# One PSUM tensor per bank in place of one per two banks, in a linear-attention and mixture-of-experts kernel

**Chip, cores, metric.** One core of a Trainium2 chip. The metric is the device time of one execution in microseconds (us). Before the change three runs gave 286.63 to 290.11 us, median 289.97. Every run here carries the profiler's records of span and clock, so nothing in this document tells how the kernel runs without them.

## The reference, cut to what matters

```python
# attention with a decaying state; r, k, v, w of shape (4, 8, 768, 48)
for t in range(S):
    y[:, :, t] = r_t @ (state + (u * k_t) outer v_t)
    state = w_t[..., None] * state + k_t outer v_t
x = y as 3072 tokens of 384
# every token to one of 8 experts, highest logits first, each expert full at 384 tokens
logits = x @ w_gate
...
for e in range(E):
    h = maximum(x[mask] @ w1[e], 0)          # 384 -> 1024
    out[mask] = h @ w2[e]                    # 1024 -> 384
```

## The kernel before

The attention runs in 24 units of 128 tokens (about 20 to 165 us). The experts follow in two passes: 256 tokens each, from a token list made while the last attention units still run, and then 128 tokens each. For every 128 tokens GpSimd issues an indirect DMA that gathers rows (L1076), and later one that scatters results (L1168). It also issues the weight loads (L1024, L1026). TensorE turns the gathered rows (L1087), multiplies by w1 (up, L1117), ScalarE (in the second pass also VectorE) applies the ReLU (L1134, L1132), TensorE multiplies by w2 (down, L1148), and the result is copied out of PSUM (L1161, L1158). Four PSUM banks go round among up and down products. They are the halves of two tensors, which the attention uses first:

```python
    Cps = ps.tile([128, 1024], FP32, name="cps", tag="cps")        # two banks
    Gps = ps.tile([128, 2, 512], FP32, name="gps", tag="gps")      # two banks: the grams
    # ... (cut) the attention: grams by TensorE, then masks by VectorE
                    mm(Gps[cols, cc, j * 64:(j + 1) * 64], lhsT=t[rows, j, 0, cols],
                       rhs=t[rows, j, 1, cols], start=True, stop=True)
                nc.vector.copy_predicated(out=M[slot(("m", u))][:, cc], mask=...,
                    data=Gps[:, cc, :256].rearrange("p (j t) -> p j t", j=NPAIR))
    # ... (cut) the experts
        views = {"T": list(Tps), "D": [Yps[:, 0], Yps[:, 1]],
                 "B": [Cps[:, :512], Cps[:, 512:], Gps[:, 0], Gps[:, 1]]}
    # ... (cut) up, ReLU, down, copy; self.bank("B", key) is one of the four
                            nc.tensor.matmul(
                                self.bank("B", b[1])[:, i * size:(i + 1) * size],
                                lhsT=w1sb[:, k, f8 * 128:(f8 + 1) * 128], rhs=xv()[:, k],
                                start=(k == 0), stop=(k == 2))
                        nc.scalar.activation(out=to, in_=of, func=AF.Relu)
    # ... (cut)
                    got = nc.gpsimd.indirect_dma_start(
                        out=self.xg[slot[xg[1]]], out_offset=None, in_=self.x_dram,
                        in_offset=bass.IndirectOffsetOnAxis(ap=tok[:, j:j + 1], axis=0))
```

Of the kernel before, what the change touches and what calls it, by code (L numbers as in the profile page):

```python
# [8 lines left out]
FP32 = mybir.dt.float32  # L9
# [8 lines left out]
B, H, S, D = 4, 8, 768, 48  # L18
# [4 lines left out]
E = 8  # L23
# [4 lines left out]
NPAIR = 4  # L28


def _bc(ap, n, pos=None):

    pat = [list(x) for x in ap.ap]
    pat.insert(len(pat) if pos is None else pos, [0, n])
    return bass.AP(tensor=ap.tensor, offset=ap.offset, ap=pat)


def _free(ap, *pattern):

    return bass.AP(tensor=ap.tensor, offset=ap.offset,  # L40
                   ap=[list(ap.ap[0])] + [list(x) for x in pattern])
# [38 lines left out]
class Line:  # L80
# [10 lines left out]
    def add(self, name, u, *a, **kw):  # L91
        op = Op(name, u, *a, **kw)
        self.ops.append(op)
        self.op[name, u] = op
        return op
# [176 lines left out]
FREE = {"LG": -2, "LE": -2, "LT": -2, "LF": -2}  # L272


def _attention(tc, inp, sb, ps, r, k, v, w, uu, wg, x_dram, negl, consts, stores):

    nc = tc.nc
    NB = 2
# [27 lines left out]
    Wd = tiles(sb, "wd", 2, [128, NPAIR, B])  # L306
    LS = tiles(sb, "ls", 2, [128, 128])

    Cps = ps.tile([128, 1024], FP32, name="cps", tag="cps")
    Tps = [ps.tile([128, 512], FP32, name=f"tps{i}", tag=f"tps{i}") for i in range(2)]  # L310
    Tb = [t.bitcast(BF16) for t in Tps]
    Gps = ps.tile([128, 2, 512], FP32, name="gps", tag="gps")
    Yps = ps.tile([128, 2, 512], FP32, name="yps", tag="yps")

    Cx = Cps[:, 128:896].rearrange("p (x n) -> p x n", x=2)
# [3 lines left out]
    def mm(*a, **kw):  # L319
        ln.last = nc.tensor.matmul(*a, **kw)  # L320
# [16 lines left out]
    def zero(name, i, engine, ns, ap):  # L337
# [5 lines left out]
    zw = [zero("Zw", i, "POOL", 150, t[:, :, D:]) for i, t in enumerate(Ws)]  # L343
    zs = zero("Zs", 0, "POOL", 500, St[0])
    zg = [add("Zg", i, "DVE", 300,
              lambda i=i: nc.vector.memset(Gps[32:64 if i == 0 else 128, :, 256:448]
                                           if i == 0 else Gps[96:128, :, 256:448], 0.0))
          for i in range(2)]
    zy = [add("Zy", i, "DVE", 400,
              lambda i=i: nc.vector.memset(Yps[32 + 64 * i:64 + 64 * i, :, :256], 0.0))  # L350
# [77 lines left out]
    for u in range(NU):  # L428
# [4 lines left out]
        def cum(ww=ww, b=b):  # L433
# [31 lines left out]
            give=[("dg", u)],  # L465
# [5 lines left out]
        for half in range(2):  # L471
# [11 lines left out]
            def ev(u=u, half=half):  # L483
# [6 lines left out]
                give=[("t", u, half)], **kw)  # L490

        def state(u=u, vv=vv, b=b):
            s = KR[slot(("kr", u))]
            for j in range(NPAIR):
                for half, cc in ((0, 0), (1, 1), (0, 1), (1, 0)):
                    h = 2 * j + cc
                    rows = slice(half * 64, half * 64 + 64)
                    mm(Gps[cc * 64:cc * 64 + D, half, 256 + j * D:256 + (j + 1) * D],
                       lhsT=s[rows, 0, h, :D],
                       rhs=vv[rows, b, h * D:(h + 1) * D], start=True, stop=True)  # L500

# [2 lines left out]
            take=("G", ("gu", u)), give=[("kr", u)])  # L504

        def u_of(half):
            return Gps[:112, half, 256:256 + NPAIR * D].rearrange("p (j d) -> p j d", d=D)

        add("SM", u, "DVE", 357, after=[op["U", u], get("SW", u - B), zs],
            take=("Sm", ("sm", u)), give=[("gu", u)],  # L510
            fn=lambda u=u, c=c, b=b: nc.vector.tensor_tensor(
                out=Sm[slot(("sm", u))][:112], in0=u_of(0), in1=St[c % 2][:112, b],
                op=ALU.add))
        if not last_c:
            add("SP", u, "DVE", 357, after=[op["SM", u]], take=("Sp", ("sp", u)),
                give=[("gu", u)],
                fn=lambda u=u: nc.vector.tensor_tensor(
                    out=Sp[slot(("sp", u))][:112], in0=u_of(1),
                    in1=Sm[slot(("sm", u))][:112], op=ALU.add))
            add("SW", u, "POOL", 600, after=[op["SP", u], op["WE", c * B + B - 1],  # L520
                                            get("Y1", u - B)],
                give=[("sp", u)],
                fn=lambda u=u, c=c, b=b: nc.gpsimd.tensor_tensor(
                    out=St[(c + 1) % 2][:112, b], in0=Sp[slot(("sp", u))][:112],
                    in1=_free(Wd[c % 2][:112, 0, b:b + 1], [B, NPAIR], [0, D]),
                    op=ALU.mult))
# [19 lines left out]
        def gram(u=u):  # L546
            t = KRT[slot(("krt", u))]
            for j in range(NPAIR):
                for cc, half in ((0, 0), (1, 1), (0, 1), (1, 0)):
                    rows, cols = slice(cc * 64, cc * 64 + D), slice(half * 64, half * 64 + 64)  # L550
                    mm(Gps[cols, cc, j * 64:(j + 1) * 64], lhsT=t[rows, j, 0, cols],
                       rhs=t[rows, j, 1, cols], start=True, stop=True)
        add("G", u, "PE", 580, gram, mode="Q", lag=120, take=("G", ("g", u)),
            after=krt_ops + [op["IA", u]])
        for cc in range(2):
            add(f"MS{cc}", u, "DVE", 440, after=[op["G", u], op["DG", u]], give=[("g", u)],
                fn=lambda u=u, cc=cc: nc.vector.copy_predicated(  # L557
                    out=M[slot(("m", u))][:, cc], mask=_free(mask, [0, NPAIR], [1, 64]),
                    data=Gps[:, cc, :256].rearrange("p (j t) -> p j t", j=NPAIR)))

        for cc in range(2):
            def intra(u=u, vv=vv, b=b, inter=inter, cc=cc):
# [13 lines left out]
                give=[("m", u), ("krt", u), ("sm", u)] if cc else ())  # L576
# [39 lines left out]
        if b == B - 1:  # L616
            def logits(c=c):
# [8 lines left out]
                give=[("xf", u - i) for i in range(B)])  # L626
# [43 lines left out]
EARLY = 20  # L670
# [8 lines left out]
class Deal:  # L679
# [98 lines left out]
    def early(self, tok, a1, *after):  # L778


        nc, c = self.nc, self.c
        last = self.own(0, EARLY, *after)
        nm2 = self.t("fm", [128, NTILE, E])
        non = self.t("non", [128, NTILE, E], BF16)
        m8, m8b = self.t("m8", [96, 2, 8]), self.t("m8b", [(EARLY - GI) * E, 8])
        (wa, wb), (num, end) = self.worst([(m8[:, 0], 0, GI), (m8b, GI, EARLY)], "T", last,
                                          sums=EARLY)
        self.early_worst = wa
        ready = self.V(EARLY * E, lambda: nc.vector.scalar_tensor_tensor(
            out=nm2[:, :EARLY], in0=non[:, :EARLY], scalar=BIG, in1=self.nl[:, :EARLY],  # L790
            op0=ALU.mult, op1=ALU.add), last)
        key = self.key()
        mean = lambda: self.bank("T", key)[:E, :8]

        def means():
            for i, (of, rows) in enumerate(((m8[:, 0], GI * E), (m8b, (EARLY - GI) * E))):
                nc.tensor.matmul(mean(), lhsT=c["mean8"][:rows], rhs=of, start=(i == 0),
                                 stop=(i == 1))
        p = self.P(130, means, wa, wb, take=("T", key))
        pen, cut, q1 = self.t("pen8", [E, 8]), self.t("cut", [E, 8]), self.t("q1", [E, 1])  # L800
        v = self.V(8, lambda: nc.vector.tensor_scalar(
            out=pen, in0=c["steps"], scalar1=num, scalar2=float(EARLY * 128 - KEEP + 10),
            op0=ALU.add, op1=ALU.is_gt), end)
        v = self.V(8, lambda: nc.vector.scalar_tensor_tensor(
            out=cut, in0=pen, scalar=BIG / 2, in1=mean(), op0=ALU.mult, op1=ALU.add), v, p,
            give=[key])
        v = self.V(8, lambda: nc.vector.tensor_reduce(out=q1, in_=cut, axis=AX.X,
                                                      op=ALU.min), v)
        qb, key, p = self.bound(q1, "T", v)
        asg = self.t("asg", [128, NTILE, E], BF16)  # L810
        v = self.tt(asg[:, :EARLY], nm2[:, :EARLY], lambda: _bc(qb(), EARLY, 1), ALU.is_le, p,
                    ready, give=[key], n=EARLY * E)
        return self.slots(asg, a1, EARLY, FIRST, tok, "T", v)

    def slots(self, asg, mine, n, size, tok, pool, *after, verify=None):
# [575 lines left out]
def kernel(  # L1391
# [12 lines left out]
    nc = tc.nc  # L1404
    x_dram = nc.dram_tensor("x_scratch", (N, DX), BF16, kind="Internal").ap()
# [3 lines left out]
    inp = ctx.enter_context(tc.tile_pool(name="inputs", bufs=1))  # L1409
# [4 lines left out]
    negl = keep.tile([128, NTILE, E], FP32, name="negl", tag="negl")  # L1414
# [9 lines left out]
    with ExitStack() as work, tc.manual_schedule():  # L1424
        nc.scalar.preload_act_table_set("natural_log_exp_and_others")
        consts, later = _constants(tc, const)
        sb = work.enter_context(tc.tile_pool(name="work", bufs=1))
        ps = work.enter_context(tc.tile_pool(name="psum", bufs=1,
                                             space=bass.MemoryType.PSUM))
        stores = []  # L1430
        line, ins, (Cps, Tps, Gps, Yps) = _attention(
            tc, inp, sb, ps, r, k, v, w, u, moe_w_gate, x_dram, negl, consts, stores)
        op = line.op
        fixed = line.plan(lambda o: o.u * PERIOD + AT[o.name])
        assert fixed, "the keys lead to a deadlock"
# [32 lines left out]
        for i, (engine, ns, fn) in enumerate(later):  # L1468
# [2 lines left out]
        line.pools.update(B=4, D=2, FXG=Experts.XG, FXE=Experts.XE, FHS=Experts.HS,  # L1471
                          FOS=Experts.OS)
        views = {"T": list(Tps), "D": [Yps[:, 0], Yps[:, 1]],
                 "B": [Cps[:, :512], Cps[:, 512:], Gps[:, 0], Gps[:, 1]]}

        def bank(pool, key):
            return views[pool][line.slot[key]]
        deal = Deal(nc, line, bank, sb, consts, negl, "D", 20 * 16)
        deal.flag = flag
        zero = deal.step("POOL", 200, lambda: nc.gpsimd.memset(a1[:, EARLY:], 0.0))  # L1480
# [31 lines left out]
    with tc.If(more > 0):  # L1512
        tok = keep.tile([128, NTILE], I32, name="tok", tag="tok")
        with ExitStack() as a:
            sb = a.enter_context(tc.tile_pool(name="b_sb", bufs=1))
            ps = a.enter_context(tc.tile_pool(name="b_ps", bufs=1,
                                              space=bass.MemoryType.PSUM))
            line = Direct()
# [38 lines left out]
```

## Time and profile before

| | before |
|---|---|
| three timed runs | 289.97, 286.63, 290.11 us |
| profiled run | 272.1 us (span 270.2, mean clock 0.933) |
| TensorE busy | 81% of the span; no other engine over 55% |
| first pass of the experts | 168.1 to 237.4 us |
| second pass | 237.4 to 262.3 us |

The last two rows run, to within 0.4 us, from the first up product to the last down product of a pass. Keep an eye on the first two: the profiled run is 18 us shorter than the timed ones. The prediction shows the lines.

### The profile page before, as it was taken

Reading aid. Unit: us, or ns where it says so; the run is one execution under the profiler, and the core shown is the slowest. Engines: PE = TensorE matmul, PEld = TensorE weight load, DVE = VectorE, ACT = ScalarE, POOL = GpSimd, SP = SyncE. Lnnn points to the kernel's source line nnn. Section 1 sums busy time; section 2 is a strip of 40 time slices with the busy share of each in tenths; the row PEclk is TensorE's granted clock in tenths of the full one; section 3 lists DMA queues with packets and bytes.
Section 4 is the critical chain, followed back from the end, with each engine's and each line's share of the span. In section 5 each row is a group of like instructions: output and inputs, shape, how many; then the busy total and the mean of one; then the engine's idle time right before and its main releaser. Section 6 shows DMA issues by size and latency. Waiting matters only on the chain.

```text
span 270.2 us, 10431 instructions
## 1 busy us (share of the span) xinstructions
PE 219.8 (81%) x4469; PEld 162.0 (60%) x4469; DVE 144.9 (54%) x438; ACT 131.9 (49%) x248; POOL 148.4 (55%) x180
## 2 busy tenths in 40 slices
PE   2089998898999799879679589888887789899980
PEld 0057766676677587657467367465555656577850
DVE  6846675575667566555387861264543383024440
ACT  2137676575677577556445223374444454542300
POOL 7425577455757557845735358164752452776331
PEclk9999999999999999997799755599999999999995
DMA  7957799678869769999997994996999599443111
GB/s 155 192 116 135 144 177 202 120 153 182 177 127 205 155 128 196 197 202 138 168 220 142 182 163 83 207 194 151 184 177 225 112 202 187 120 142 105 58 65 63
DMA packets 118388, 42.24 MB, mean 156 GB/s; under 512 B 101440, under 2 KB 113728, under 8 KB 118336
## 3 DMA queue, kind: packets, MB, share of 16 engines
q1 hardware_dynamic: 104128, 21.84, 40.0%
q0 software_dynamic: 14208, 19.66, 38.3%
q8 instruction: 37, 0.61, 0.9%
q14 instruction: 15, 0.12, 0.1%
HBM read 46.61 MB, written 7.47 MB: 200 GB/s over the span
## 4 chain that ended last, share of the span: by engine, by line
PE 66%; issue 11%; DVE 10%; ACT 6%; POOL 4%; POOLq 0%; DVEq 0%; ACTq 0%
PE yps L320 12%; PE gps L320 8%; PE cps L320 6%; PE tps L320 6%; PE gps L1117 6%; PE cps L1117 6%; PE tps L478 5%; PE cps L1148 5%; PE gps L1148 5%; ACT Fhs L1134 3%; DVE mm L557 3%; PE tps L590 2%; POOL out_dram L1168 2%; DVE Dohl L870 1%; PE tps L1087 1%
## 5 line engine op out<-in xcount | busy, mean ns | idle before, releaser
L466 POOL TENSOR_TENSOR mm<-diag,dd 128x512 f32<-128x512 f32 x24 | 25.1, 1046 | 59.0 <-DVE dd L461 23.0
L484 ACT COPY krT<-tps 112x512 f32<-112x512 f32 x48 | 28.1, 586 | 26.5 <-PE tps L478 23.5
L1168 POOL DMA_INDIRECT out_dram<-Fos,tok x24 | 24.1, 1005 | 24.3 <-ACT Fos L1161 11.5
L1076 POOL DMA_INDIRECT Fxg<-x_scratch,tok x24 | 23.4, 975 | 22.4 <-PE tps L1087 12.0
L320 PE MATMUL cps<-ww,negut 128*128 128x384 f32 x48 | 23.7, 579 | 12.3 <-issue 7.2
L478 PE MATMUL tps<-ident,krs 128*112 128x128 f32 x192 | 32.2, 295 | 0.6 <-DVE Dboth L710 0.6
L557 DVE COPY_PREDICATED mm<-mask,gps 128x256 f32<-128x256 uint8 x48 | 18.7, 442 | 22.1 <-PE gps L320 16.3
L478 PEld LDWEIGHTS tps<-ident,krs 128*112 128x112 f32 x192 | 23.0, 142 | 11.1 <-issue 6.1
L1148 PEld LDWEIGHTS <-Fhs 128*128 128x128 bf16 x192 | 17.8, 97 | 13.0 <-issue 3.5
L453 POOL TENSOR_TENSOR rku<-kr 128x384 f32<-128x384 f32 x24 | 24.0, 1002 | 2.6 <-DMA kr<-in_r_dram 2.6
L457 POOL TENSOR_TENSOR rku<-rku,u_bc 128x384 f32<-128x384 f32 x24 | 24.0, 1002 | 2.4 <-DMA u_bc<-in_u_dram 2.4
L320 PE MATMUL yps<-mm,vv 64*48 64x64 f32 x768 | 20.5, 234 | 4.9 <-issue 3.2
L320 PE MATMUL yps<-krT,sm 48*48 48x64 f32 x384 | 22.2, 233 | 1.9 <-issue 1.8
L447 DVE TENSOR_TENSOR krs<-kr,cps 128x768 f32<-128x768 f32 x24 | 22.7, 945 | 1.6 <-ACT cps L442 1.6
L320 PEld LDWEIGHTS yps<-mm,vv 64*48 64x48 f32 x768 | 15.0, 127 | 13.7 <-DVE mm L557 5.9
L578 ACT COPY xf<-yps 128x512 f32<-128x512 f32 x24 | 14.0, 582 | 16.8 <-PE yps L320 12.6
L320 PE MATMUL yps<-krT,st 48*48 48x64 f32 x384 | 21.9, 233 | 0.0
L442 ACT ACTIVATE cps<-cps 128x768 f32<-128x768 f32 x24 | 19.3, 804 | 5.2 <-DVE cps L438 5.2
L1117 PEld LDWEIGHTS <-w 128*128 128x128 bf16 x192 | 15.7, 103 | 9.2 <-issue 6.3
L1134 ACT ACTIVATE Fhs<-cps 128x512 bf16<-128x512 f32 x20 | 11.9, 597 | 18.1 <-PE cps L1117 17.9
L1134 ACT ACTIVATE Fhs<-gps 128x512 bf16<-128x512 f32 x20 | 11.9, 597 | 14.6 <-PE gps L1117 14.4
L320 PEld LDWEIGHTS yps<-krT,sm 48*48 48x48 f32 x384 | 15.6, 128 | 4.8 <-issue 3.6
(200 smaller groups left out, 473.8 us busy)
## 6 DMA issues: line engine op xcount, KB each, us to landing
w<-in_moe_w_dram POOLq DMA_DIRECT2D x8, 768.0 KB
ww<-in_w_dram SPq DMA_DIRECT2D x24, 192.0 KB, 3.7
kr<-in_k_dram SPq DMA_DIRECT2D x24, 192.0 KB, 3.8
kr<-in_r_dram SPq DMA_DIRECT2D x24, 192.0 KB, 4.1
vv<-in_v_dram SPq DMA_DIRECT2D x24, 192.0 KB, 3.8
kr<-in_moe_w_dram POOLq DMA_DIRECT2D x4, 768.0 KB
x_scratch<-row SPq DMA_DIRECT2D x7, 384.0 KB, 4.8
vv<-in_moe_w_dram POOLq DMA_DIRECT2D x2, 768.0 KB
```

The lines of the kernel that those rows point to most:

```text
L320: ln.last = nc.tensor.matmul(*a, **kw)
L453: fn=lambda u=u, kr=kr, b=b: nc.gpsimd.tensor_tensor(out=P[slot(("p", u))], in0=kr[:, b, 0, :], in1=kr[:, b, 1, :], op=ALU.mult))
L457: fn=lambda u=u: nc.gpsimd.tensor_tensor(out=P[slot(("p", u))], in0=P[slot(("p", u))], in1=u_bc, op=ALU.mult))
L466: fn=lambda u=u: nc.gpsimd.tensor_tensor(out=M[slot(("m", u))], in0=_free(diag, [0, 2], [0, NPAIR], [1, 64]), in1=_free(Dg[slot(("dg", u)) ...
L478: ln.last = nc.tensor.transpose(t[:112, at:at + 128], pair_of(s[:, x], j), ident)
L484: nc.scalar.copy(out=KRT[slot(("krt", u))][:112, 2 * half:2 * half + 2].rearrange("p j x t -> p (j x t)"), in_=Tps[slot(("t", u, half))][: ...
L557: fn=lambda u=u, cc=cc: nc.vector.copy_predicated(out=M[slot(("m", u))][:, cc], mask=_free(mask, [0, NPAIR], [1, 64]), data=Gps[:, cc, :25 ...
L1076: got = nc.gpsimd.indirect_dma_start(out=self.xg[slot[xg[1]]], out_offset=None, in_=self.x_dram, in_offset=bass.IndirectOffsetOnAxis(ap=to ...
L1117: nc.tensor.matmul(self.bank("B", b[1])[:, i * size:(i + 1) * size], lhsT=w1sb[:, k, f8 * 128:(f8 + 1) * 128], rhs=xv()[:, k], start=(k == ...
L1134: nc.scalar.activation(out=to, in_=of, func=AF.Relu)
L1148: nc.tensor.matmul(self.bank("B", b[1])[:, :DX], lhsT=hv()[:, f8, h * 128:(h + 1) * 128], rhs=w2sb[:, f8, :], start=(f8 == 0), stop=(f8 == ...
L1168: put = nc.gpsimd.indirect_dma_start(out=self.out, out_offset=bass.IndirectOffsetOnAxis(ap=tok[:, j:j + 1], axis=0), in_=self.os[slot[o[1] ...
```

## The change

The built program orders every access to a tensor, so a ReLU that reads bank 0 of `Cps` stands between two groups of products into bank 1. The change gives every bank a tensor of its own. The two halves of `Cps` are used as one by the attention, so that tensor lives in a pool that is closed when the experts first ask for a bank, and two one-bank tensors take its place.

```diff
-    Cps = ps.tile([128, 1024], FP32, name="cps", tag="cps")
+    Cps = pc.tile([128, 1024], FP32, name="cps", tag="cps")
-    Gps = ps.tile([128, 2, 512], FP32, name="gps", tag="gps")
+    Gps = [ps.tile([128, 512], FP32, name=f"gps{i}", tag=f"gps{i}") for i in range(2)]
 ... (every Gps[x, cc, y] becomes Gps[cc][x, y]; a key's name and the pools' set-up are cut)
         views = {"T": list(Tps), "D": [Yps[:, 0], Yps[:, 1]],
-                 "B": [Cps[:, :512], Cps[:, 512:], Gps[:, 0], Gps[:, 1]]}
+                 "B": [None, None] + Gps}
         def bank(pool, key):
-            return views[pool][line.slot[key]]
+            i = line.slot[key]
+            if views[pool][i] is None:
+                wide.__exit__(None, None, None)
+                new = work.enter_context(psum("psum_c2"))
+                views[pool][:2] = [new.tile([128, 512], FP32, name=f"cps{x}", tag=f"cps{x}")
+                                   for x in range(2)]
+            return views[pool][i]
```

## The prediction

> **What bounds the kernel now.** I read the table of the page first (TensorE busy 81%, no other engine over 55%), then busy time by stage, then the waits inside the stage that looked loose, then the chain that ended last, in that stage.
>
> ```profile
> core 0: us, PE busy (x) PEld busy (x) DVE busy (x) ACT busy (x) POOL busy (x), PEclk, DMA share, GB/s
> 20.00:135.00 115.00, 103.68 (x3052) 79.50 (x3051) 69.61 (x167) 74.70 (x139) 72.53 (x84) 0.97 0.85 165
> 135.00:167.00 32.00, 25.10 (x646) 19.69 (x644) 21.31 (x72) 11.72 (x24) 16.64 (x19) 0.76 0.88 163
> 167.00:200.00 33.00, 27.65 (x187) 17.95 (x186) 14.85 (x69) 15.62 (x31) 17.38 (x19) 0.87 0.98 180
> 200.00:235.00 35.00, 29.18 (x249) 20.16 (x248) 14.59 (x72) 16.56 (x32) 16.30 (x18) 1.00 0.90 171
> 235.00:252.00 17.00, 16.36 (x188) 12.59 (x187) 6.02 (x11) 5.76 (x11) 11.42 (x12) 1.00 0.36 116
> ```
>
> The attention (20 to 135) keeps TensorE busy 90% of the time. The experts come in two passes: 256 tokens each (about 168 to 237), where TensorE stands still for 11.2 of 68 us, and 128 tokens each (from 238), where it hardly stands still at all (16.36 of 17). So the first pass is where something can be won. Its waits, from 167 to 252:
>
> ```profile
> ACT Fhs L1134 <- PE cps L1117: 13.1, 16, 2.4
> ACT Fhs L1134 <- PE gps L1117: 13.0, 17, 2.3
> ...
> PE cps L1117 <- ACT Fhs L1134: 3.0, 4, 0.7
> PE gps L1117 <- ACT Fhs L1134: 2.9, 4, 0.7
> ...
> PE gps L1117 <- ACT Fos L1161: 1.5, 3, 0.6
> ...
> PE cps L1148 <- ACT Fhs L1134: 1.5, 3, 0.6
> ...
> PE cps L1117 <- ACT Fos L1161: 1.2, 2, 0.6
> ...
> PE gps L1148 <- ACT Fhs L1134: 0.8, 2, 0.6
> ```
>
> TensorE waits for ScalarE 18 times, 10.9 us in all: nearly all of its idle time. ScalarE in turn waits for TensorE, and has only 32.2 us of work in those 68. Neither is short of capacity; they take turns. First two lines of the timeline there (start, length, engine, instructions), then three of the chain (start, length, what), show one such turn:
>
> ```profile
> 203.12 1.15 PE L1117 MATMUL cps<-Fxe,kr 128*128 128x256 bf16 x9
> ...
> 204.37 0.60 ACT L1134 ACTIVATE Fhs<-cps 128x512 bf16<-128x512 f32 x1 [0.39 <-PE cps L1117]
> ```
> ```profile
> 203.29 1.00 PE cps L1117 x9
> ...
> 204.37 0.61 ACT Fhs L1134
> ...
> 205.01 0.49 PE cps L1117 x3
> ```
>
> Nine matmuls are six that fill one bank and three for half of the next bank; then the ReLU of the first bank; then the other three. With four banks there should be no such turn.
>
> **What the Trainium skill says.** "PSUM — Partial Sum Buffer", section "PSUM bank collisions raise a hardware error", says that two engines collide only in the same bank and quadrant, that accesses to different banks run clean, and that a semaphore is to guard a bank. So a wait of TensorE on a read of the neighbouring bank guards nothing; the trace shows such waits, 10.9 us of them. "Perfetto Trace Analysis", section "Matmuls", wants independent groups to rotate through banks so that the evacuation of one lies beside the next group's matmuls; the schedule rotates over four, but the chain shows no overlap. "DMA: Bandwidth & Descriptors", section "Anatomy of one DMA — SWDGE (gpsimd) path", fits 2.0 us plus bytes over 436 GB/s: for one weight load here (384 x 1024 fp32, 1.57 MB read) an estimate of 5.6 us. The trace agrees: the packets of one load span 5.0 to 7.1 us.
>
> **The change part by part.** Built side by side, both programs have the same instructions in the same order on every engine, except that VectorE has four small memsets of the gram banks for two. What differs is who waits for whom.
>
> Start: the two memsets took 378 ns each; four halves cost at most some 0.3 us more, at the beginning of VectorE's queue. Estimate +0.2.
>
> Attention: the grams and state products alternate between the two banks, so the last matmuls into both are neighbours. The masks (MS0) and state sums may now start one matmul earlier, some 30 ns (32 matmuls in 0.85 us), and are followed by the same wait one instruction later. VectorE gets 27 waits more. The one gram wait that moves (on the state sum) moves by one matmul. Estimate 0.
>
> First pass: in the program of before, the second half of a bank's products waits for the ReLU or copy of the other bank of the same tensor, and that ReLU waits for the first half. In the changed one it waits only for its own bank, last used four groups ago. The down products (L1148), which belong to the expert before, waited for the last ReLU of the current one and now wait for a ReLU three ScalarE instructions earlier. All 18 waits are of these two kinds, so 10.9 us go. Each also drains the pipeline: nine matmuls in 1.15 us with 0.27 for one are (1.15 - 0.27) / 8 = 0.11 apart, so the next could have started at 204.11 where it started at 205.01. That is 0.90 lost where 0.74 is shown as idle; 0.16 x 18 = 2.9 more. Sum 13.8 us out of the pass's 69.3.
>
> Check by work: an expert has 24 up products at 0.11 (2.64), 16 down products at (1.46 - 0.326) / 7 = 0.162 (2.59), six transposes at 0.055 (0.33) and a round of the token assignment between them (0.31 + 0.40 + 0.42 = 1.13): 6.7 us. Now an expert takes 9.4 (192.33 to 201.70 to 211.11). ScalarE has 4 x 0.60 + 4 x 0.48 = 4.3 per expert, about 4.7 with gaps, so it keeps up with 6.7.
>
> Second pass: 3.0 us per expert (243.79 to 246.79) with TensorE full. Its cross-bank waits go as well, but they end before TensorE arrives. Estimate 0. The tail after the last matmul (262 to 270) is unchanged.
>
> **The rivals, which eat part of the 13.8.**
>
> Weights. Eight loads for experts 4 to 7 run from 178.7 to 231.6, their packets covering 46.6 us of it, at a DMA share of 0.9 or more. Today they are issued by GpSimd in step with TensorE and start about 2 us after issue; the last lands at 231.6 and is used at 234.81. If TensorE is 13.8 earlier it wants it at 221.0, but starting at about 178 with no gap between them, 178 + 46.6 = 224.6. That is a new wait of 3.6 us, on the DMA. For: shares of 0.98 and 0.90. Against: idle gaps at 185 to 187 and 213 to 215. If the DMA could not be compressed at all, the gain would be only 234.81 - 231.6 = 3.2 us, and the time 287.
>
> Token assignment. Its small matmuls sit in TensorE's order, so TensorE waits if VectorE isn't done. A round needs about 2.55 (L723 to L755), 1.75 (to L966) and 2.6 or 1.9 (back to L723): 6.9 or 6.2 against the 6.7 of work. Today VectorE waits for TensorE in it. I take off 1.0 us in all.
>
> GpSimd. From 228 to 248 it issues gathers and scatters without a pause, 1.28 us each, and begins when the second token list is ready, itself late in the assignment. The transposed rows of the second pass could come up to 1 us late. I take off 0.5. If gathers queue behind weight loads it would be 3 or more.
>
> ScalarE as the new bound is the fourth; 4.7 against 6.7 speaks against it, and it would leave a gain above 10.
>
> **Range and chances.** 13.8 - 3.6 - 1.0 - 0.5 + the start's -0.2 = 8.5, rounded to 9 because the overlapped loads at 215 to 231 took 5.5 each and not 5.8. The timed runs (289.97) are some 18 us longer than the profiled one (272.1); I assume that the gain carries over whole, since the wait is ScalarE's latency and not TensorE's speed: 289.97 - 9 = 281.0. All of the rivals at their worst leave about 3 (287), none of them 14 (276). Range 276.0 to 286.0. Two per cent is 5.8 us, a time under 284.2. Faster 0.75, within 2% 0.23, slower 0.02: no wait is added that takes the place of a shorter one.
>
> **What would show it.** Right: no waits of TensorE for Fhs or Fos in the first pass (under 2 us of 10.9); six, not nine, matmuls before a ReLU; expert period near 6.9; new waits of TensorE on weights, at experts 6 or 7; the pass shorter by 8 to 11; the attention and the second pass within 1 us each. Wrong: the pass still near 69 because the DMA or the assignment fills the holes (then waits on weights or VectorE of over 8 us), or a shorter pass whose gain is lost before the second pass because the second token list or its gathers are late, or a granted clock that falls where TensorE is fuller (1.00 from 176 to 264 now).

## The result, and the profile after

The changed kernel took 266.54, 266.9, 270.41 and 264.71 us, median 266.72; the kernel before, in the same rounds, a median of 288.3. The ratio is 0.9344 [0.9166, 0.9522]. (A run counts as slow when it is over 1.5% above the fastest of its kernel. Here and below a ratio is the mean time of one kernel's fast runs over that of the other's fast runs of the same rounds, so not quite the ratio of the medians quoted.) That is 21.6 us less in the medians and 18.7 less in the means of the fast runs. The prediction had 9 and held 14 for out of reach.

Profile against profile the change looks much smaller: 272.1 us before, 266.54 after. These rows give the two passes: window, length, then busy us and count of TensorE, its weight loads, VectorE, ScalarE and GpSimd, then clock, DMA share, GB/s. Before:

```profile
168.10:237.40 69.30, 58.30 (x443) 38.75 (x441) 29.30 (x139) 32.50 (x63) 34.67 (x37) 0.95 0.92 174
237.40:262.30 24.90, 24.12 (x282) 18.60 (x279) 10.60 (x20) 7.07 (x13) 12.96 (x14) 1.00 0.29 97
```

After:

```profile
171.40:227.30 55.90, 53.11 (x445) 37.39 (x443) 28.93 (x139) 32.00 (x63) 33.34 (x36) 1.00 1.00 197
227.30:256.80 29.50, 25.49 (x281) 19.01 (x279) 10.49 (x19) 7.08 (x13) 13.67 (x15) 0.94 0.23 81
```

The first pass is 13.4 us shorter, close to the 13.8 that the waits promised. (In part that is luck: the first expert of before took 9.2 us in this profile, where the pass had a clock of 0.95, and 6.6 in a later profile of the same kernel at 1.00.) But the pass starts 3.3 us later and the second takes 4.6 us more; TensorE is idle for 4.0 of its 29.5. All 18 waits for ScalarE in the first pass are gone. What TensorE waits for in that pass now (us in total, times, longest):

```profile
PE gps L1117 <- DMA vv<-in_moe_w_dram: 1.6, 1, 1.6
PE yps L966 <- DVE Dmm L710: 1.0, 1, 1.0
```

And the turn of nine, ReLU, three has become six for one bank, with the next twelve under the ReLU (the timeline after: start, length, engine and instructions):

```profile
204.07 0.82 PE L1117 MATMUL cps<-Fxe,vv 128*128 128x256 bf16 x6
...
204.73 1.47 PE L1117 MATMUL gps<-Fxe,vv 128*128 128x256 bf16 x12
204.99 0.60 ACT L1134 ACTIVATE Fhs<-cps 128x512 bf16<-128x512 f32 x1 [0.19 <-PE cps L1117]
```

So the mechanism was the predicted one. Two things were not explained: where the timed runs of before spend the 18 us that its profile does not show, and why the change takes some of them away.

### The profile page after: what moved, and what is told of

It is laid out like the page before. It is cut to its first block, busy times and chain, and to the rows that moved or that the text cites. A ratio compares the mean times of both kernels' runs of the same rounds, so it can differ in the third digit from the quotient of the medians.

```text
span 264.6 us, 10437 instructions
## 1 busy us (share of the span) xinstructions
PE 215.1 (81%) x4469; PEld 160.1 (61%) x4469; DVE 142.9 (54%) x440; ACT 131.3 (50%) x248; POOL 148.6 (56%) x180
## 4 chain that ended last, share of the span: by engine, by line
PE 68%; DVE 8%; DMA 8%; issue 7%; another core or an unknown queue 3%; ACT 3%; POOL 2%; POOLq 0%; DVEq 0%
PE yps L320 11%; PE tps L478 8%; PE gps L320 7%; PE tps L320 7%; PE cps L320 7%; PE gps L1117 6%; PE gps L1148 6%; PE cps L1117 6%; PE cps L1148 5%; DMA vv<-in_moe_w_dram 4%; DMA ww<-in_w_dram 3%; PE tps L590 2%; PE tps L1087 1%; DVE Dohl L870 1%
## 5 line engine op out<-in xcount | busy, mean ns | idle before, releaser
L466 POOL TENSOR_TENSOR mm<-diag,dd 128x512 f32<-128x512 f32 x24 | 25.1, 1048 | 57.5 <-DVE dd L461 31.1
L1168 POOL DMA_INDIRECT out_dram<-Fos,tok x24 | 24.1, 1003 | 24.7 <-DVE Fos L1158 13.7
L1076 POOL DMA_INDIRECT Fxg<-x_scratch,tok x24 | 23.5, 977 | 20.3 <-PE tps L1087 11.1
L557 DVE COPY_PREDICATED mm<-mask,gps 128x256 f32<-128x256 uint8 x48 | 18.7, 442 | 27.9 <-PE gps L320 16.7
L478 PE MATMUL tps<-ident,krs 128*112 128x128 f32 x192 | 31.5, 290 | 0.6 <-DVE Dboth L710 0.6
L478 PEld LDWEIGHTS tps<-ident,krs 128*112 128x112 f32 x192 | 22.7, 140 | 10.9 <-issue 6.2
L320 PE MATMUL yps<-mm,vv 64*48 64x64 f32 x768 | 19.9, 232 | 9.0 <-DVE mm L557 6.0
L1148 PEld LDWEIGHTS <-Fhs 128*128 128x128 bf16 x192 | 17.8, 99 | 11.9 <-issue 2.8
L320 PE MATMUL yps<-krT,sm 48*48 48x64 f32 x384 | 21.6, 229 | 1.1 <-issue 1.1
L320 PE MATMUL yps<-krT,st 48*48 48x64 f32 x384 | 21.3, 228 | 0.3 <-issue 0.3
L320 PE MATMUL gps<-krT 48*64 48x64 f32 x768 | 18.4, 227 | 1.0 <-issue 1.0
L1134 ACT ACTIVATE Fhs<-cps 128x512 bf16<-128x512 f32 x20 | 11.8, 598 | 13.8 <-PE cps L1117 10.3
L1117 PEld LDWEIGHTS <-w 128*128 128x128 bf16 x192 | 15.1, 100 | 5.8 <-issue 4.1
```

Source lines behind the costliest of these rows:

```text
L320: ln.last = nc.tensor.matmul(*a, **kw)
L466: fn=lambda u=u: nc.gpsimd.tensor_tensor(out=M[slot(("m", u))], in0=_free(diag, [0, 2], [0, NPAIR], [1, 64]), in1=_free(Dg[slot(("dg", u)) ...
L478: ln.last = nc.tensor.transpose(t[:112, at:at + 128], pair_of(s[:, x], j), ident)
L1076: got = nc.gpsimd.indirect_dma_start(out=self.xg[slot[xg[1]]], out_offset=None, in_=self.x_dram, in_offset=bass.IndirectOffsetOnAxis(ap=to ...
L1117: nc.tensor.matmul(self.bank("B", b[1])[:, i * size:(i + 1) * size], lhsT=w1sb[:, k, f8 * 128:(f8 + 1) * 128], rhs=xv()[:, k], start=(k == ...
L1148: nc.tensor.matmul(self.bank("B", b[1])[:, :DX], lhsT=hv()[:, f8, h * 128:(h + 1) * 128], rhs=w2sb[:, f8, :], start=(f8 == 0), stop=(f8 == ...
```

## The experiments

Fifteen runs were made, in four sets, each on one chip with runs of the kernel before in the same rounds.

| set | chip | kernel before, median (runs) |
|---|---|---|
| 1 | 15 | 286.07 us (11) |
| 2 | 11 | 269.0 us (11) |
| 3 | 2 | 289.51 us (7) |
| 4 | 10 | 288.02 us (7) |

The chips differ as much as the kernels do; that became the key to the case. Medians here and below include slow runs; where times are subtracted, the means of fast runs are used. The kernel before has 283.6, 265.8, 286.4 and 286.6 us in the four sets by that measure. The profiles of before_sp, b_burst, after_third, b_burst_again and pause_all are of slow runs.

### Set 1: where the 18 us are, and which half of the change counts

Theory A: the extra time of the timed runs lies outside the first pass. Rival B: it lies in the first pass, whose waits are longer than in the one profile.

**b_again**, the kernel before, unchanged, profiled once more.

> The kernel before, unchanged, once more. Its three early runs took 287 to 290 us but its profiled run only 272, while the changed kernel's runs and its profile agree (265 to 270). Theory A (the gain is the cross-bank waits of the first expert pass, about 13.5 us in the traces, and the rest of the 21.6 us is a slower condition of the kernel before that its one profile missed): the runs spread over 270 to 290 and a profile near 285 shows extra time outside the first pass, or a lower granted clock. Rival B (the waits cost more in the timed runs than in the profile): a profile near 285 shows the same stages, with the first pass near 78 us and not 69.

284.13 us, 0.9924 [0.9816, 1.0033] of itself in other runs, so a difference of 1% means nothing here. Its two passes:

```profile
172.50:240.30 67.80, 55.43 (x443) 37.54 (x441) 29.29 (x139) 32.02 (x62) 33.98 (x37) 1.00 0.86 167
240.30:274.50 34.20, 26.43 (x283) 20.16 (x280) 10.59 (x19) 7.55 (x14) 12.86 (x14) 0.90 0.19 64
```

The first pass is as in the first profile (67.8 against 69.3); the second takes 34.2 us, not 24.9, and the pass begins 4.4 us later. A holds, B falls. So the first profile of before was not typical of what was timed.

**exp_only, att_only, c_only**: the banks split for the experts' products only, in the attention only, or only `Cps` for the experts.

```diff
 exp_only:  +    Gps2 = pg.tile([128, 2, 512], FP32, name="gps", tag="gps")   # attention as before
            +                 "B": [None, None, None, None]}                 # four new tensors
 att_only:  +                 "B": [Cps[:, :512], Cps[:, 512:], None, None]}
            +                views[pool][2:] = [two[:, 0], two[:, 1]]         # one tensor again
 c_only:    +    Gps2 = ps.tile([128, 2, 512], FP32, name="gps", tag="gps")
            +                 "B": [None, None] + Gps}                       # halves of Gps2
```

> One tensor per bank for the experts' products only; the grams of the attention keep their two-bank tensor. Theory A: the whole gain, ratio to the kernel before 0.93 to 0.94, 265 to 269 us, first pass 56 us. Rival C (the split in the attention gives a part, for instance because masks and state sums start earlier): ratio 0.96 or above.

> One tensor per bank for the grams of the attention only; the experts use two-bank tensors as before. Theory A: nothing, ratio 0.995 to 1.005, 285 to 290 us, with the 18 waits of TensorE for ScalarE in the first pass as before. Rival C: a ratio of 0.98 or below.

> Only the cumulative-sum tensor is split into two banks for the experts; the gram tensor stays one of two banks throughout. Half of the 18 waits are on each tensor (9 each, 5.7 us on the one and 5.2 us on the other, drains included 7.1 and 6.7). Theory A: about half of the first pass's gain, a pass of 61 to 64 us, ratio about 0.965. If an engine other than ScalarE's turn-taking bounded the pass, one half alone would give nearly all (pass under 59) or nearly nothing (over 67).

| | median us | ratio | first pass | second pass |
|---|---|---|---|---|
| b_again | 284.13 | 0.9924 | 67.8 | 34.2 |
| exp_only | 269.6 | 0.9513 [0.9439, 0.9588] | 59.6 | 28.6 |
| att_only | 281.05 | 0.9851 [0.9750, 0.9953] | 68.1 | 31.2 |
| c_only | 277.63 | none given | 62.1 | 31.1 |

The split for the experts' products gives most of it, though exp_only missed all three of its figures (0.93 to 0.94, 265 to 269 us, a pass of 56). Its first pass ran at a mean clock of 0.94, and the full change was not run on this chip, so what it lacks, if anything, is not known. `Cps` alone takes 5.7 us off the first pass, about half of the 11.9 that separate b_again and after there. The split in the attention leaves the first pass alone (68.1); its 1.5%, which lies between the two forecasts, is hardly more than the kernel before differs from itself.

### What the stalls look like

In b_again TensorE, VectorE and ScalarE stand still together twice: before the first pass and where the passes meet. At the first place VectorE's mask waits for the last gram of the attention. First profile of before, VectorE's timeline (in brackets the idle time before, and what ended it):

```profile
160.75 0.77 DVE L557 COPY_PREDICATED mm<-mask,gps 128x256 f32<-128x256 uint8 x2 [1.44 <-PE gps L320]
```

The same line of b_again, and then its gram on TensorE's timeline:

```profile
166.86 0.78 DVE L557 COPY_PREDICATED mm<-mask,gps 128x256 f32<-128x256 uint8 x2 [7.87 <-remote]
```

```profile
159.15 1.49 PE L320 MATMUL gps<-krT 48*64 48x64 f32 x25
160.90 0.48 PE L320 MATMUL gps<-krT 48*64 48x64 f32 x4 [0.26 <-issue]
161.61 0.49 PE L320 MATMUL gps<-krT 48*64 48x64 f32 x3 [0.23 <-issue]
```

The 32 products, one stretch of 1.10 us in the first profile of before, come in steps, and the last ends at 162.1 by the profile; but the trace's record of TensorE's semaphore has the update for it at 166.77. "Perfetto Trace Analysis", section "Summary: the profiler window per engine type", says that TensorE's reported end is an estimate; here the signal comes 4.7 us after that estimate, which is why the releaser is only called "remote". Call a product late by the time from its reported end to the first update of its semaphore from then on. In the first profile of before none of the 331 products that raise it is more than 0.5 us late. In b_again nine are late by more than 1 us, the worst by 4.7, 3.5 and 2.8; in after fourteen, the worst by 4.9 and 3.9. What goes on meanwhile is on GpSimd's timeline of b_again:

```profile
158.12 1.05 POOL L1076 DMA_INDIRECT Fxg<-x_scratch,tok  x1 [0.32 <-DVE tok L890]
159.48 0.98 POOL L1076 DMA_INDIRECT Fxg<-x_scratch,tok  x1 [0.30 <-issue]
...
165.46 0.83 POOL L1024 DMA_DIRECT2D w<-in_moe_w_dram  x1
166.26 0.96 POOL L1026 DMA_DIRECT2D w<-in_moe_w_dram  x1
```

Eight issues in one string; the late semaphore comes during the last. In after the string ends at 165.45 and the semaphore comes at 165.1. The ten profiled traces of this study that have late products have 106 of them over 1 us. For 82, GpSimd was issuing a DMA during more than half of the time by which they were late. That alone proves little: GpSimd issues DMAs in about half of the time from 156 to 262 us, and stretches of the same lengths put there at random would give 62. By the section just named, such a line shows the generation of descriptors, not the transfer. "SBUF — State Buffer", section "Who interferes with whom", knows only VectorE and GpSimd as rivals for a port, and gives TensorE ports of its own; so what is seen here is not on that page.

A caution on the counts. These ten traces lack updates: b_again has 327 of TensorE's semaphore, 368 of VectorE's and 220 of ScalarE's, the first profile of before 333, 376 and 228. A product whose own update is missing is counted up to the next one. The 106 share 70 updates, and if each update is given to the last product before it, 22 stay late by over 1 us, the gram among them. So the counts here and below are upper bounds. VectorE's long wait for the gram does not hang on them.

Theory S: strings of GpSimd's issues hold TensorE up. Rival T: the transfers themselves do, or TensorE's instruction loads, or the clock.

### Set 2, chip 11: nothing is late

**after_again** is the changed kernel, unchanged. **before_sp** and **after_sp** are both kernels with every gather and scatter as a plain DMA of as many bytes from SyncE's queue; a small load of the token list ahead of the first gather of a pass keeps the order of time. The results are wrong on purpose.

```diff
-                    got = nc.gpsimd.indirect_dma_start(
-                        out=self.xg[slot[xg[1]]], out_offset=None, in_=self.x_dram,
-                        in_offset=bass.IndirectOffsetOnAxis(ap=tok[:, j:j + 1], axis=0))
+                    if not j:
+                        nc.sync.dma_start(out=self.tk, in_=tok[:, :1])
+                    n = (j // 2) * 6 + 4 + j % 2 if dve else (j // 5) * 6 + j % 5
+                    got = nc.sync.dma_start(out=self.xg[slot[xg[1]]],
+                                            in_=self.x_dram[n * 128:(n + 1) * 128, :])
```

**b_burst** is the kernel before with four more small gathers in a gap of GpSimd's.

```diff
+        def burst(load):                       # load: the w1 load of expert 6
+            load()
+            for t in idle:                     # four tiles of 128x64 bf16, read by nobody
+                nc.gpsimd.indirect_dma_start(
+                    out=t, out_offset=None, in_=x_dram.rearrange("n (a b) -> (n a) b", b=64),
+                    in_offset=bass.IndirectOffsetOnAxis(ap=tok1[:, :1], axis=0))
```

> The changed kernel, unchanged, on another occasion. Both theories: 264 to 270 us, 0.92 to 0.95 of the kernel before, whose own runs lie at 281 to 290 us. In the profile of every run of this study but the first of the kernel before, TensorE's semaphore is raised 1 to 5 us after the modelled end of some products (last gram 4.9 us late in the profile after), each time while GpSimd issues indirect DMAs one behind the other; in the first profile of the kernel before no product is over 0.5 us late. Theory S (GpSimd's strings of issues hold TensorE up): the late products come back here at the same places, 20 to 30 us late in sum over all waits and about 10 us of it on the path. Rival T (an accident of those traces): they come at other places or not at all.

> The kernel before, with every gather of token rows and every scatter of results replaced by a plain DMA of as many rows and bytes from SyncE's queue; the result is wrong on purpose. GpSimd then issues the weight loads alone. Theory S (GpSimd's strings of indirect issues hold TensorE up): no product's semaphore comes over 1.5 us late, VectorE's 7.9 us wait at 157 to 166 us falls to about 1.5, the second pass falls from 34 to 25 us, and the kernel takes 266 to 272 us, 14 to 20 less than the kernel before in the same rounds. Rival T (the rows that land, TensorE's instruction loads or the clock hold it up): the bytes stay, so the late products stay and the time is 280 to 287 us.

> The changed kernel with the same replacement; wrong on purpose. Theory S: no product over 1.5 us late, first pass 54 to 56 us, second 24 to 25 us, 252 to 259 us in all, so 12 to 15 us less than before_sp: what the change gives where nothing holds TensorE up, near the 13.8 us that I read from the first profile's waits, and less than the 17 to 20 us that it gives between the two kernels themselves. Rival T: 262 to 268 us, 18 to 20 less than before_sp.

> The kernel before with four more gathers, of 128 rows of 128 bytes into tiles that nobody reads, put behind the load of expert 6's first weights, where GpSimd has been idle for 5.5 us (206 to 212 us in its own trace). Theory S: they make a string of six issues there, and one or two products of TensorE at that place, where none was late before, have their semaphore raised 2 to 4 us late; the first pass grows from 68 to 70 to 72 us and the kernel by 2 to 4 us. Rival T: GpSimd had the time to spare and 64 KB more land, so no product there is late and the time stays within 0.5 us.

| chip 11 | median us | ratio | late over 1 us |
|---|---|---|---|
| before | 269.0 | | (not profiled) |
| after_again | 256.79 | 0.9555 [0.9403, 0.9706] | 0 |
| before_sp | 267.1 | 0.9945 [0.9817, 1.0074] | 0 |
| after_sp | 253.25 | 0.9519 [0.9396, 0.9643] | 0 |
| b_burst | 272.15 | 1.0153 [0.9989, 1.0317] | 0 |

On this chip the kernel before is as fast as its first profile and no product is late in the four profiles, strings or not; nor does any of them lack updates. The expectation of after_again (264 to 270 us) missed, because I had taken the hold-up for a property of the kernel. The others decide nothing about S. But the set shows the change by itself. The passes of after_again:

```profile
167.70:222.10 54.40, 52.81 (x443) 37.11 (x441) 28.77 (x139) 32.44 (x63) 35.25 (x38) 1.00 1.11 222
222.10:245.60 23.50, 22.97 (x283) 18.36 (x280) 10.58 (x19) 7.07 (x13) 13.06 (x14) 1.00 0.30 102
```

And those of b_burst, which has all the waits of before for ScalarE (11.2 us against 10.9) and, unlike the first profile of before (clock 0.95), the full clock all through:

```profile
170.90:237.50 66.60, 55.29 (x443) 37.54 (x441) 29.25 (x139) 32.50 (x63) 39.01 (x42) 1.00 0.97 182
237.50:262.50 25.00, 24.23 (x282) 18.68 (x280) 10.58 (x19) 7.07 (x13) 13.03 (x14) 1.00 0.28 97
```

At equal clock and without late products the change takes 12.2 us off the first pass and 1.5 off the second. (From before_sp to after_sp it is 16.4 and 1.5, but there the first pass of before_sp had a clock of 0.95.) TensorE's new waits in the first pass of after_again are these two:

```profile
PE gps L1117 <- DMA vv<-in_moe_w_dram: 1.1, 1, 1.1
PE gps L1117 <- DMA kr<-in_moe_w_dram: 0.4, 1, 0.4
```

### Set 3, chip 2: the same kernels where products are late

> The changed kernel once more. The last four kernels ran on chip 11, and there no product of TensorE was late in any trace and the kernel before took 269 us; on chip 15 it took 286 us with late products in every trace. So the hold-up goes with the chip. If this chip is of the slow kind (kernel before at 280 us or more): 0.92 to 0.945, 264 to 270 us, late products at 160, 182, 197, 223 and 230 to 237 us. If it is of the other kind: 0.945 to 0.96, 252 to 260 us, no late product.

> The kernel before with plain DMAs from SyncE's queue in place of every gather and scatter; wrong on purpose. On chip 11, which does not hold TensorE up, it was the kernel before's equal (0.9945), so the replacement in itself costs and gains nothing. On a chip of the slow kind, theory S (GpSimd's strings of indirect issues hold TensorE up there): 266 to 272 us, 13 to 20 less than the kernel before, no product over 1.5 us late, second pass 25 us. Rival T (the rows that land or TensorE's instruction loads, which stay): 280 to 287 us and late products as in the kernel before. On a chip of the other kind: 0.98 to 1.01, and nothing is told.

> The changed kernel with the same replacement; wrong on purpose; 253.3 us on chip 11. On a chip of the slow kind, theory S: 251 to 258 us, 12 to 16 less than before_sp_again, and 9 to 14 less than the changed kernel itself. Rival T: 262 to 268 us, as the changed kernel itself. On a chip of the other kind: 251 to 256 us.

> The kernel before with four more gathers that nobody reads, where GpSimd is idle. On chip 11 it took 1.0153 [0.9989, 1.0317] of the kernel before, with no late product. On a chip of the slow kind, theory S: one or two products at 205 to 212 us have their semaphore raised 2 to 4 us late where the kernel before has none, and the first pass grows by 2 to 4 us over the 68 us of the kernel before. Rival T: none late there, first pass 67 to 69 us.

| chip 2 | median us | ratio | late over 1 us (worst) |
|---|---|---|---|
| before | 289.51 | | (not profiled) |
| after_third | 269.82 | 0.9434 [0.9251, 0.9617] | 13 (5.0) |
| before_sp_again | 268.28 | 0.9425 [0.9245, 0.9605] | 0 |
| after_sp_again | 252.84 | 0.8893 [0.8723, 0.9063] | 0 |
| b_burst_again | 285.55 | 0.9918 [0.9615, 1.0220] | 9 (4.7) |

This speaks for S and against T as it was put. With GpSimd's indirect issues gone and the bytes still moved, both kernels are as fast on chip 2 as on chip 11 (267.1 and 253.25 there), none of the products is late, and VectorE waits for the gram as briefly as in the first profile. VectorE's timeline of before_sp_again:

```profile
158.71 0.77 DVE L557 COPY_PREDICATED mm<-mask,gps 128x256 f32<-128x256 uint8 x2 [1.44 <-PE gps L320]
```

In the means of fast runs the replacement takes 286.4 - 268.5 = 17.9 us off the kernel before and 269.3 - 253.5 = 15.8 us off the changed one (in medians, slow runs included, 21.2 and 17.0). On chip 11, where nothing is held up, it is worth 1.4 and 1.6 us, so some of both is not the hold-up. What this does not separate: the replacement takes away GpSimd's issue and also the transfer of rows picked one by one, since one block of rows is moved in their place. GpSimd's 16 plain weight loads stay, and with these alone nothing is late.

b_burst_again puts strings where there were none. On TensorE's timeline of b_again one wait at that place is

```profile
214.06 0.49 PE L1117 MATMUL cps<-Fxe,vv 128*128 128x256 bf16 x3 [0.61 <-ACT Fos L1161]
```

and in b_burst_again, whose first pass began 2.1 us later and had lost more by then,

```profile
219.37 0.49 PE L1117 MATMUL cps<-Fxe,vv 128*128 128x256 bf16 x3 [1.37 <-ACT Fos L1161]
```

behind two products that are 1.7 and 1.4 us late by the same update; b_again has none late between 203 and 231. So the added issues do harm as S expects, but less than I had written (2 to 4 us late): the wait grew by 0.8 us. The first pass takes 71.1 us against 67.8, as forecast, but that is luck: 2.4 of the 3.3 us are its first expert, which comes before the added issues and ran at a lower clock. The first expert of b_again and of b_burst_again (the last three numbers are clock, DMA share, GB/s):

```profile
172.50:179.10 6.60, 5.52 (x47) 3.67 (x45) 3.79 (x20) 3.48 (x8) 2.22 (x4) 1.00 0.87 186
174.60:183.70 9.10, 8.29 (x47) 4.73 (x46) 3.72 (x19) 3.53 (x8) 2.10 (x3) 0.60 0.51 116
```

The sixth expert, where the added issues lie, took 9.7 us against 8.9. On the whole time the interval is too wide to show 2 or 3 us, and the median even went the other way.

### Set 4, chip 10: does a pause free TensorE?

What stayed open was whether each issue holds TensorE up for itself (P) or TensorE is held until GpSimd has nothing left to issue (Q). **pause_six** puts four small memsets, 1.0 us together, ahead of each of the last five of the first six gathers; **pause_all** puts two ahead of every gather and scatter. **after_fourth** is the changed kernel as control. Results are right in all three.

```diff
+                    if not dve and 1 <= j <= 5:            # pause_all: always, and range(2)
+                        for i in range(4):
+                            nc.gpsimd.memset(self.rest, float(i))
                     got = nc.gpsimd.indirect_dma_start(
```

> The changed kernel as the control of the two that follow. On a chip of the slow kind (kernel before at 280 us or more) 264 to 271 us, the last gram at about 160 us late by 4.7 to 5 us and products late in the strings of GpSimd's issues after it; on a chip of the other kind 252 to 260 us and none late.

> The changed kernel with four small memsets of GpSimd (0.2 us each in the profile before, so 0.8 us) ahead of each of the last five of the six gathers that GpSimd issues in one string at 156 to 164 us; nobody reads their tile, the result is right. On a chip of the slow kind, theory P (each issue holds TensorE up for itself, and a pause lets it catch up): the last gram is late by at most 1.5 us in place of 4.9, VectorE's wait for it falls from 8 to 2 to 4 us, the first pass begins 3 to 5 us earlier, and the kernel takes 260 to 267 us. Theory Q (TensorE is held until GpSimd has nothing left to issue): the gram stays late until the end of the string, now 4 us later, and the kernel is 3 to 4 us slower than the control. On a chip of the other kind: within 1 us of the control.

> The changed kernel with two such memsets (0.4 us) ahead of every gather and every scatter. On a chip of the slow kind, theory P: products late by over 2 us are rare or gone, and the kernel takes 256 to 265 us, if the 0.4 us that each of 48 issues takes longer does not bring the gathers of the second pass late (that would be 4 to 6 us of waits of TensorE for Fxg at 230 to 240 us, and would eat the gain). Theory Q: late products as in the control, and 268 to 278 us. On a chip of the other kind: 0 to 5 us slower than the control.

| chip 10 | median us | ratio | late over 1 us (worst) | first pass begins |
|---|---|---|---|---|
| after_fourth | 268.44 | 0.9358 [0.9199, 0.9518] | 15 (4.8) | 172.0 |
| pause_six | 265.86 | 0.9290 [0.9204, 0.9376] | 9 (3.6) | 167.6 |
| pause_all | 273.67 | 0.9457 [0.9277, 0.9636] | 1 (1.3) | 171.0 |

VectorE's wait for the gram in after_fourth:

```profile
165.82 0.78 DVE L557 COPY_PREDICATED mm<-mask,gps 128x256 f32<-128x256 uint8 x2 [7.93 <-remote]
```

and in pause_six:

```profile
161.13 0.78 DVE L557 COPY_PREDICATED mm<-mask,gps 128x256 f32<-128x256 uint8 x2 [1.09 <-PE gps L320]
```

P's forecast came true: the gathers go on until 171 us, but with pauses between them the gram is not late and the pass begins 4.4 us earlier. In all eight traces with late products and without pauses the last gram is 4.7 to 4.8 us late; in pause_six and pause_all it is under 0.1. The test is narrow: the gram of pause_six ended at 161.0, before the second gather began (161.38), and a pause spaces out the transfers as well as the issues. pause_all takes nearly all lateness away and is 2.8 us slower than its control in fast runs, though the intervals overlap; its profile, of a slow run, shows GpSimd's own transfers late. TensorE's waits in pause_all from 171 to 255 us:

```profile
PE gps L1121 <- DMA kr<-in_moe_w_dram: 5.9, 1, 5.9
PE tps L1091 <- DMA Fxg<-x_scratch,tok: 5.2, 3, 2.0
```

I had put down the second (4 to 6 us) and not the first. pause_six is 1.8 us below its control in fast runs, but the intervals overlap, so that it is faster is not shown; it was not run on a chip like 11.

**Left open.** By what path GpSimd's indirect DMAs hold TensorE up, and whether it is their issue or their transfers; whether TensorE itself or its signal is late, since updates of VectorE and ScalarE are missing in the same traces; whether recording the profile has a part in it, a rival that no run tests; why chips 2, 10 and 15 do it and chip 11 does not. Which chip the first profile of before ran on is not recorded.

## Why the prediction was right or wrong, point by point

- **The 18 waits and the 13.8 us: right.** They are all gone, six matmuls precede a ReLU where nine did, and the period is 7.0 to 7.2 us for 6.9 foreseen (third to sixth expert of after_again; the last two, where the waits for weights fall, 8.5 and 8.7). At equal clock and without late products the first pass lost 66.6 - 54.4 = 12.2 us net, and with the 1.5 us of new waits for weights 13.7 gross. That this meets 13.8 so closely is partly luck: the plain-DMA kernels lost 15.2 and 16.4 net, with a clock of 0.95 before. c_only says the same by halves.
- **What was taken off, 5.3 us: a step that failed.** The weights were to cost 3.6 us, at 221.0 wanted and 224.6 landed. Where nothing is late they cost 1.5: the packets of the eight loads ran from 178.9 to 219.3, 40.4 us and not 46.6 (each alone still spans 5.0 to 6.5), at 222 GB/s in the pass where before had 174. I had taken the time that the loads' packets covered before as what they need; they overlap more when they are issued closer together. Of the assignment's 1.0 nothing is seen in after_again, and in after one wait of 1.0 just behind a string that held TensorE up. GpSimd's 0.5 is not seen either.
- **Second pass 0: off by 1.5 us** (25.0 to 23.5) without late products. TensorE had looked full; its busy time itself fell by 1.3.
- **So the change alone is worth 11 to 15 us, not 8.5:** in fast runs 11.4 on chip 11, 11.5 between the plain-DMA kernels there, 14.9 between them on chip 2.
- **"The timed runs (289.97) are some 18 us longer than the profiled one (272.1); I assume that the gain carries over whole": the other step that failed.** I took the 18 us for a constant that the change does not touch. They are the hold-up, on chips where it happens, and the gain is not the same with them and without: in fast runs 11.4 us on chip 11, but 17.1 on chip 2 and 18.9 on chip 10. Where it grows is not shown. On chip 2 the replacement took 17.9 us off before and 15.8 off after, a difference of 2 us from three or four runs each. In the traces the place seemed to be the second pass: 34.2 us in b_again, 29.5 in after, 24.9 and 23.5 undisturbed. But 2.3 of b_again's 9.3 us more are longer busy time, at a clock of 0.90, and att_only (31.2) and b_burst_again (30.7), whose experts have the waits of before, lie close to the 30.6 of after_third. So that the changed kernel is hurt less where the passes meet does not follow.
- **The sum.** Predicted 8.5. With 1.5 us taken off in place of 5.3 it would have been 12.3, which is about what chip 11 shows and inside the range. The 5 to 7 us from there to the 17.1 to 18.9 of the held-up chips, and to the 18.7 of the first comparison, come with the hold-up and are not accounted for further.
- **The rivals.** GpSimd was on the list, for the right stretch (228 to 248 us, "without a pause"), but as a cause of late gathers, which would have made the gain smaller. Its effect on TensorE itself could not be read from a trace in which it did not happen. That "none of them 14" set the low end was an argument from the rivals alone; a range that allowed for not knowing the 18 us would have been wider on both sides.

## What to carry to other kernels

In this program two-bank tensors that two engines share serialise banks that have nothing to do with each other; the waits of TensorE on the reader of the other bank, plus the drain of each, told nearly what a split gives (13.8 read; 13.7 measured at equal clock). When the profiled run and the timed runs differ by 18 us, the profile is of another situation than the one that is timed, and until it is known where the difference lies, neither may be added to the other. Take the trace apart before a longer stretch is put down to a cause: a lower clock in one expert can look like the effect that was forecast. Where products end late by their semaphores and not by their reported ends, look at what GpSimd issues in that moment, and try a pause in strings that are not urgent.

## What the Trainium skill lacked or had wrong

- "SBUF — State Buffer", section "Who interferes with whom", calls the port pair of VectorE and GpSimd the only contention. On chips 2, 10 and 15 TensorE's products were signalled up to 5.0 us late while GpSimd issued DMAs in a string, and on chip 2 plain DMAs from SyncE in their place made the kernel 17.9 us faster in fast runs. No page was found that has this; that a port is what they contend for is not shown.
- No page was found to say that chips differ for one and the same program: the kernel before took 269.0 us on chip 11 and 286.1 to 289.5 on three others.
- "Perfetto Trace Analysis", section "Summary: the profiler window per engine type", says that TensorE's end is estimated, but not how far the signal can come behind it: 4.7 to 5.0 us for the last gram, 0.5 at most where nothing was held up.
